# Fewer key loads, a mask built in two parts, and three moved steps in a fused decay-attention and soft-MoE kernel

## The chip, the cores and the metric

The kernel runs on one core of one Trainium2 chip. The metric is device time in microseconds, the median of several runs; lower is better.

## What is computed

Two stages follow each other. The first is block-wise linear attention with a decay `lam` of each head (batch 4, 8 heads, 768 positions, head width 64). The second is a soft mixture of experts over the 3072 tokens that come out of it (width 512, 32 slots, 8 experts of 4 slots, hidden width 1024).

```python
for b in range(nb):                       # blocks of 64 positions
    intra = einsum('bhic,bhjc->bhij', qb, kb) * Dmask          # Dmask: lam**(i-j), i >= j
    intra = einsum('bhij,bhjd->bhid', intra, vb)
    inter = einsum('bhid,bhde->bhie', qb * lam_pow, kv_state)
    out[:, :, sl] = intra + inter
    kv_state = lam_block * kv_state + einsum('bhsd,bhse->bhde', kb * rev_pow, vb)
x = out.transpose(0, 2, 1, 3).reshape(3072, 512)
logits = x @ phi                                               # 512 x 32
d = softmax(logits, over tokens);  slot_input = d.T @ x
h = relu(slot_input[e] @ w1[e]);   slot_out[e] = h @ w2[e]     # each expert e
y = softmax(logits, over slots) @ slot_out
```

## The kernel before, in words

The kernel works in chunks of 128 positions: 6 a batch element (`NB`), 24 in all (`T`). One loop over `t` (line 541) handles all of them, and every engine keeps the order in which the program issues (`InOrder`, line 52).

A chunk has three loads of 256 KB: queries and keys turned (`qT`, `kT`, head width on the partitions) and values (`vN`). Some chunks have a fourth, the keys with positions on the partitions (`kN`). `loaded(t)`, line 37, says which: before the change chunks 2, 3, 4 of every six, and 7 and 19, 14 in all. The last chunk of every six needs no such keys. For the six others `turn_k` (line 307) makes them on the chip: four TensorE transpositions of `kT` into a PSUM bank and a ScalarE copy (`kn`).

Iteration `t` issues from SyncE (SP) the loads of chunk `t+2` and, between them, part of the weight stream: 16 slabs of `w1` of 1 MB, and `w2` in nine slabs of 1 MB (`w2p`) and 28 pieces of 256 KB (`w2t`), the latter into buffers that the chunk loop no longer needs. The chunk loads share a ring of 12 buffers (`ld`).

For chunk `t` the work is:

- `scores(t)`: TensorE, keys by queries, into two banks; 8 products of 128x128 where `whole(t)`, else 16 smaller ones that leave out the upper half and store the diagonal blocks exchanged.
- `masks(t)`: VectorE multiplies the banks by the decay mask (`at`). The mask tile has six places a half: four ordinary ones, and two exchanged ones (places `HP` and `HP+1`) that only chunks which aren't `whole` read, the first of them chunk 5. `powers_of` (line 211) fills a place by a VectorE scan.
- `recall(t)`: TensorE, old state by decayed queries (`qs`, made on GpSimd by `decay_q`).
- `attend(t)`: TensorE, values by `at`, on top of `recall`; ScalarE copies the two halves out (`xt`).
- `state(t)`: TensorE, decayed keys (`kd`, made on GpSimd by `decay_k`, one buffer) by values into bank `kv`; VectorE adds the decayed state (`st`). `decay_state` on GpSimd decays it for the next chunk (`dec`).
- `natural(t)`: four TensorE transpositions of `xt` and a ScalarE copy (`x`), done for two chunks at every even `t`.
- every four chunks `logits`, `weights`, `slots` and `slot_softmax`: running softmax over the tokens.

A chunk that opens a batch element (`opens`, t = 0, 6, 12, 18) runs `state` ahead of `attend`, as odd chunks do; other even chunks run it behind. At the last chunk (`last`) a few extra products end the token softmax.

Behind the loop come the experts: `first(0)` and `first(1)` (`w1` slabs, 32 products of 512 columns each for a half of the experts and each of two banks), `second(0, ...)` and `second(1, ...)` (`w2`, for the two halves of the output columns), and `put`: a product, a copy by ScalarE or VectorE, and a 256 KB store from SP, 24 in all. The first 9 stores lie inside `second(1)`, at the places that `PUTS` names; three more of the first column half and the 12 of the second follow.

Of the kernel before, what the change touches and what calls it, by code (L numbers as in the profile page):

```python
# [16 lines left out]
NB = S // P  # L17
T = B * NB
HP = H // 2
# [16 lines left out]

def loaded(t):

    return t % NB in (2, 3, 4) or t in (7, 19)


def whole(t):
# [25 lines left out]
def decay_attn_soft_moe(  # L68
# [23 lines left out]
    def bank(tag):  # L92
        return ps.tile([P, 512], F32, tag=tag, name=tag)
# [6 lines left out]
    d = const.tile([P, P], F32, name="d")  # L100
# [3 lines left out]
    def load_chunk(t, which=(0, 1, 2, 3)):  # L104
        srcs = (qT, kT, vN, kN)
        for i in which:
            if i == 3 and not loaded(t):
                continue
            tl = loads.tile([P, 512], F32, tag="ld", name="ld")
            sp.dma_start(out=tl, in_=srcs[i][t])  # L110
            IN[t, i] = tl
# [15 lines left out]
    def load_one(pool_, tag, bufs, n=1):  # L127

        t_ = pool_.tile([P, n, 512], F32, tag=tag, name="w2t", bufs=bufs)
        for m in range(n):  # L130
            Q, x, q, i = single.pop()
            sp.dma_start(out=t_[:, m], in_=rows(Q, x, q)[i])
            wt["w2", Q, q, x, i] = t_[:, m]
# [27 lines left out]
    def load_early(n):  # L161
        for _ in range(n):
            if early:
                Q, kk, q = early.pop()
                t_ = slabs.tile([P, 2, 1024], F32, tag="slab", name="slab")
                src = w1[4 * Q + q].rearrange("k p n f -> (k p n f)").rearrange("(p n y) -> n p y", p=P, n=2)
                sp.dma_start(out=t_.rearrange("p i f -> p (i f)"), in_=src[kk])
                wt["w1", Q, q, kk] = t_
            else:
                load_two()  # L170
# [40 lines left out]
    def powers_of(places, at_zero):  # L211
        for hh in range(2):
            for y in places:
                x = hh * HP + (y if y < HP else y - 2)
                dve.tensor_tensor_scan(
                    out=mask[:, hh, y, :],
                    data0=lam_sb[:, x:x + 1].broadcast_to([P, P]),
                    data1=at_zero,
                    initial=0.0,
                    op0=ALU.mult,  # L220
                    op1=ALU.add,
                )
# [78 lines left out]
    def decay_q(t):  # L301
        if t < T and t % NB > 0:
            qs = work.tile([P, HP, P], F32, tag="qs", name="qs")
            pool.tensor_tensor(out=qs, in0=IN[t, 0].rearrange("p (a b) -> p a b", a=HP), in1=qpow, op=ALU.mult)
            QS[t] = qs

    def turn_k(t, tag="kv"):

        if t < T and t % NB < NB - 1 and not loaded(t):
            tk = bank(tag)  # L310
            for hp in range(HP):
                pe.transpose(tk[:, hp * P:(hp + 1) * P], IN[t, 1][:, hp * P:(hp + 1) * P], ident)
            kn = work.tile([P, D], F32, tag="kn", name="kn")
            act.copy(out=kn, in_=tk)
            IN[t, 3] = kn
# [37 lines left out]
    def turn_v(t):  # L353

        if t < T and not whole(t):
            v_ = IN[t, 2].rearrange("p (b h c) -> p b h c", b=2, c=DH)
            for j in range(2):
                act.copy(out=vs[64 * j:64 * j + 64], in_=v_[64 - 64 * j:128 - 64 * j, :, 2:4])
# [48 lines left out]
    def decay_state(t):  # L407
        if t % NB < NB - 2:
            st = ST["st"]
            dec = work.tile([P, HP, DH], F32, tag="dec", name="dec")  # L410
            pool.tensor_tensor(
                out=dec, in0=st, in1=lamc.broadcast_to([P, HP, DH]), op=ALU.mult
            )
            ST["dec"] = dec

    def natural(t, tag="tr"):
        tr = bank(tag)
        for hp in range(HP):
            pe.transpose(tr[:, hp * P:(hp + 1) * P], XT[t][:, hp, :], ident)
        x = keep.tile([P, D], F32, tag="x", name="x", bufs=4)  # L420
        act.copy(out=x, in_=tr)
        X[t] = x
# [59 lines left out]
    def weights(raw=True):  # L482
        dp = bank("dp")
        pe.transpose(dp[:, 0:P], e, ident)
        if raw:
            pe.transpose(dp[:, P:2 * P], L, ident)
        dve.tensor_copy(out=d, in_=dp[:, 0:P])
        return dp[:, P:2 * P]
# [52 lines left out]
    for t in range(T):  # L541
        if t + 2 < T:
            load_chunk(t + 2, (0, 1))

        want = min(NSLAB, max(0, (t * PACE + AHEAD) // 100))
        load_early(want - sent)
        sent = max(sent, want)
        if t + 2 < T:
            load_chunk(t + 2, (2, 3))
        if t == 0:  # L550
            sp.dma_start(out=L, in_=phi.rearrange("p a s -> p (a s)"))

        for _ in range((2, 4, 3)[t - T + 3] if t >= T - 3 else 0):
            load_one(*ld1)
        if t == T - 1:
            load_one(work, "kd", 1)
            load_one(work, "kn", 1)
        last = t == T - 1

        asks = t // 4 - 1 if t > 0 and t % 4 == 0 else G - 1 if last else None  # L560
        sums = t // 4 - 1 if t > 4 and t % 4 == 1 else None
        if t == 0:
            turn_k(0, "tr")
            scores(0)
            scores(1)
            turn_v(0)
        elif t > 1:
            scores(t)
        masks(t)
        if last:  # L570
            ask = logits(asks)
            next(ask)

        if t % 4 == 3 or t % 4 == 0:
            next(sm, None)
        if t == T - 1:
            next(sm, None)
        opens = t % NB == 0
        if t == 0:
            decay_k(0)  # L580
            decay_q(1)
        recall(t)
        if t > 0:
            decay_q(t + 1)
        if sums is not None:
            sm = slot_softmax(sums, weights())
        if asks is not None and not last:
            ask = logits(asks)
            next(ask)
        if t % 2 == 0 and t > 0:  # L590
            turn_k(t + 1)
            natural(t - 2)
            natural(t - 1, "dp")
        elif t % NB == NB - 1:
            turn_k(t + 1)
        if sums is not None:
            next(sm)
        if asks is not None:
            next(ask)
        if last:  # L600
            natural(t - 1)
            next(ask)

            phi4 = work.tile([P, HP, 4, SL], F32, tag="carry", name="phi4")
            four = phi_sb.rearrange("p (a o) s -> p a o s", o=1)
            pool.tensor_copy(out=phi4, in_=four.broadcast_to([P, HP, 4, SL]))
        if opens or t % 2 == 1:

            state(t)
            decay_state(t)  # L610
            if t == 0:
                turn_k(1, "tr")
        attend(t)
        if last:
            cm = bank("kv")
            pe.matmul(out=cm[:, 0:4], lhsT=blk_, rhs=gm, start=True, stop=True)
            dve.tensor_reduce(out=own, in_=cm[:, 0:4], axis=AX.X, op=ALU.min)
            weights(raw=False)
        if t == 1:
            dve.tensor_reduce(out=sel, in_=ident.rearrange("p (g s) -> p s g", g=4), axis=AX.X, op=ALU.add)  # L620
            for n in range(4):
                own_ = bass.AP(
                    tensor=ident.tensor,
                    offset=ident.offset + 16 * (n // 2) + NR * (n % 2),
                    ap=[ident.ap[0], [64, 2], [40, 2], [1, NR]],
                )
                dve.tensor_reduce(out=own4[:, n:n + 1], in_=own_, axis=AX.XYZ, op=ALU.add)
            dve.tensor_reduce(out=gsel, in_=ident.rearrange("p (g s) -> p g s", g=4), axis=AX.X, op=ALU.add)
        if not opens and t % 2 == 0:
            state(t)  # L630
        decay_k(t + 1)
        if not opens and t % 2 == 0:
            decay_state(t)
        if asks is not None and not last:
            next(ask)
        if sums is not None:
            slots(sums)
        if t == 3:
            for j in range(2):
                dve.tensor_copy(out=d[:, 64 * j:64 * j + 64], in_=ident[:, 64 - 64 * j:128 - 64 * j])  # L640
            powers_of(range(HP, HP + 2), d)
        if t == 2:
            place_phi()
        if t == 2:
            pool.tensor_copy(out=blk, in_=sel.rearrange("p (o s) -> p o s", o=1).broadcast_to([P, 4, SL]))
# [302 lines left out]
```

## Time and profile before

| | |
|---|---|
| median of 3 runs | 162.91 us (162.83 to 162.95) |
| the profiled execution's own time | 162.79 us |
| its span, first to last instruction | 161.0 us |
| TensorE busy | 143.7 us (89%) |
| VectorE / ScalarE / GpSimd busy | 90.7 / 69.3 / 70.8 us |
| moved by DMA | 62.84 MB, 390 GB/s on average |
| mean granted TensorE clock | 0.972 |

Times in the rows are microseconds from the span's start. TensorE's busy time is modelled (its products are pipelined). `sc`, `gl`, `dp`, `tr`, `kv`, `xa`, `xb` are PSUM banks; a name such as `at<-sc,mask` gives the tile that is written and those that are read. All operations are recorded on line 62, that of the helper `InOrder`.

### The profile page before, as it was taken

What the parts mean: (1) busy time and instruction counts of PE and PEld (TensorE: products, weight loads), DVE (VectorE), ACT (ScalarE), POOL (GpSimd) and SP (SyncE); (2) the same over time, 40 slices, a digit from 0 to 9 for tenths busy, and PEclk for the clock granted to TensorE, in tenths of its full rate; (3) what the DMA queues carried; (4) which work ended last, traced back from release to release, by engine and by line L of the source; (5) the groups of instructions that cost most, each with busy time, mean ns of one, the idle gap of its engine ahead of it and who ended that gap; (6) DMA issues with size and microseconds to landing.
All of it is one profiled execution on the core that took longest, in us unless ns stands there. A gap on an engine that the chain in (4) does not pass through costs nothing.

```text
span 161.0 us, 5817 instructions
## 1 busy us (share of the span) xinstructions
PE 143.7 (89%) x2397; PEld 100.3 (62%) x2397; DVE 90.7 (56%) x208; ACT 69.3 (43%) x173; POOL 70.8 (44%) x102
## 2 busy tenths in 40 slices
PE   6799997999999999989999999998999999998300
PEld 6678965687668866876868686763332465647200
DVE  1956497657585566576756476565179641327500
ACT  3132325662646475634675455633035801436400
POOL 2789692357385328586057748200003893000000
PEclk9999999999999999999999999999999999999855
DMA  4999999999999999999999999999999999999993
GB/s 166 337 402 405 414 411 417 404 416 402 413 421 408 405 412 421 415 411 404 414 406 408 415 400 407 415 393 376 388 393 414 423 413 414 407 387 356 383 383 136
DMA packets 28523, 62.84 MB, mean 390 GB/s; under 512 B 2769, under 2 KB 9041, under 8 KB 26449
## 3 DMA queue, kind: packets, MB, share of 16 engines
q1 hardware_dynamic: 28352, 62.47, 100.0%
q8 instruction: 19, 0.31, 0.7%
q14 instruction: 8, 0.06, 0.1%
q10 hardware_dynamic: 144, 0.01, 0.1%
HBM read 56.17 MB, written 6.29 MB: 388 GB/s over the span
## 4 chain that ended last, share of the span: by engine, by line
PE 66%; DMA 14%; DVE 8%; issue 2%; ACT 1%; SPq 1%; POOL 1%; DVEq 0%; ACTq 0%
PE xa L62 15%; PE sc L62 14%; DMA w2p<-w_x 11%; PE xb L62 10%; PE gl L62 9%; PE kv L62 8%; PE tr L62 6%; PE dp L62 4%; DMA ld<-kT 3%; DVE mask L62 3%; DVE o L62 2%; DVE at L62 1%; SPq L62 1%; POOL kd L62 1%; DVE acc L62 0%
## 5 line engine op out<-in xcount | busy, mean ns | idle before, releaser
L62 DVE TENSOR_TENSOR at<-sc,mask 128x512 f32<-128x512 f32 x46 | 29.6, 685 | 11.2 <-PE sc L62 9.9
L62 POOL TENSOR_TENSOR qs<-ld,qpow 128x512 f32<-128x512 f32 x20 | 25.7, 1284 | 3.4 <-POOL kd L62 2.9
L62 PEld LDWEIGHTS sc<-ld 64*64 64x64 f32 (+1 forms) x608 | 19.5, 145 | 7.5 <-issue 4.2
L62 PE MATMUL sc<-ld 64*64 64x128 f32 (+2 forms) x608 | 23.1, 257 | 1.0 <-DMA ld<-kT 0.9
L62 POOL CAST ct<-part 32x256 fp32r<-32x256 f32 x26 | 10.3, 394 | 22.6 <-DVE part L62 21.5
L62 POOL TENSOR_TENSOR kd<-ld,kpow 128x512 f32<-128x512 f32 x14 | 14.7, 1050 | 8.6 <-PE kv L62 5.0
L62 PE MATMUL kv<-ld,kd 128*64 128x64 f32 x320 | 13.6, 225 | 1.1 <-issue 0.7
L62 POOL TENSOR_TENSOR dec<-st,qpow 128x256 f32<-128x256 f32 x16 | 10.1, 628 | 10.0 <-DVE st L62 10.0
L62 PEld LDWEIGHTS kv<-ld,kd 128*64 128x64 f32 x320 | 11.5, 137 | 3.5 <-issue 1.9
L62 DVE TENSOR_TENSOR st<-dec,kv 128x256 f32<-128x256 f32 x16 | 6.7, 416 | 12.1 <-PE kv L62 12.1
L62 PE MATMUL xa<-qs,st 64*64 64x128 f32 x160 | 13.3, 277 | 0.2
L62 ACT COPY xt<-xa 128x256 f32<-128x256 f32 x24 | 8.8, 366 | 10.6 <-PE xa L62 10.6
L62 POOL TENSOR_TENSOR kd<-kn,kpow 128x512 f32<-128x512 f32 x6 | 6.3, 1042 | 15.4 <-PE xb L62 10.8
L62 PE MATMUL xb<-qs,st 64*64 64x128 f32 x160 | 12.9, 278 | 0.0
L62 PE MATMUL xa<-at,ld 128*64 128x128 f32 x132 | 12.0, 283 | 1.0 <-DVE at L62 1.0
L62 ACT COPY vs<-ld 64x256 f32<-64x256 f32 x30 | 12.1, 403 | 0.7
L62 PE MATMUL xb<-at,ld 128*64 128x128 f32 x132 | 11.4, 273 | 0.0
L62 ACT COPY x<-tr 128x512 f32<-128x512 f32 (+1 forms) x13 | 7.4, 568 | 8.3 <-PE tr L62 8.1
L62 PEld LDWEIGHTS xa<-qs,st 64*64 64x64 f32 x160 | 9.0, 132 | 1.8 <-issue 0.9
L62 ACT COPY xt<-xb 128x256 f32<-128x256 f32 x23 | 8.6, 374 | 0.9
L62 ACT COPY lq<-gl 128x512 f32<-128x512 f32 (+1 forms) x6 | 3.4, 569 | 12.8 <-PE gl L62 11.9
L62 PEld LDWEIGHTS xa<-at,ld 128*64 128x64 f32 x132 | 6.8, 136 | 3.3 <-DVE at L62 1.9
(154 smaller groups left out, 273.4 us busy)
## 6 DMA issues: line engine op xcount, KB each, us to landing
slab<-w_x SPq DMA_DIRECT2D x16, 1024.0 KB, 8.7
w2p<-w_x SPq DMA_DIRECT2D x9, 1024.0 KB, 13.8
w2t<-w_x SPq DMA_DIRECT2D x28, 256.0 KB, 5.1
ld<-qT SPq DMA_DIRECT2D x24, 256.0 KB, 6.9
ld<-kT SPq DMA_DIRECT2D x24, 256.0 KB, 6.7
ld<-vN SPq DMA_DIRECT2D x24, 256.0 KB, 7.0
y<-o SPq DMA_DIRECT2D x24, 256.0 KB, 3.9
ld<-kN SPq DMA_DIRECT2D x14, 256.0 KB, 7.7
```

What stands on the lines that cost most here:

```text
L62: return self._tc.keep_in_program_order(f(*args, **kwargs))
```

## The change

Four edits.

1. `loaded(t)` names chunks 2 and 4 of every six and chunks 7 and 19: ten chunks. Chunks 3, 9, 15 and 21 get their natural keys from `turn_k` (called at `t` = 2, 8, 14 and 20, into bank `kv`), and their four loads of 256 KB are gone.
2. The exchanged mask places are filled in two parts: the two copies that make `d` move from the end of chunk 3 to that of chunk 1, place `HP` is scanned at the end of chunk 2 and place `HP+1` at the end of chunk 3.
3. At openings other than the first (t = 6, 12, 18) `decay_k(t + 1)` is issued ahead of `decay_state(t)` on GpSimd, not behind it.
4. At the last chunk `natural(t - 1)` is issued behind `weights(raw=False)`, the transposition of `e`, and not ahead of `attend`.

```diff
 def loaded(t):
-    return t % NB in (2, 3, 4) or t in (7, 19)
+    return t % NB in (2, 4) or t % (2 * NB) == 7
@@
         if last:
-            natural(t - 1)
             next(ask)
@@
         if opens or t % 2 == 1:
             state(t)
-            decay_state(t)
+            if t == 0 or not opens:
+                decay_state(t)
             if t == 0:
                 turn_k(1, "tr")
         attend(t)
@@
             weights(raw=False)
+            natural(t - 1)
@@
         if not opens and t % 2 == 0:
             state(t)
         decay_k(t + 1)
-        if not opens and t % 2 == 0:
+        if t > 0 and t % 2 == 0:
             decay_state(t)
@@
-        if t == 3:
+        if t == 1:
             for j in range(2):
                 dve.tensor_copy(out=d[:, 64 * j:64 * j + 64], in_=ident[:, 64 - 64 * j:128 - 64 * j])
-            powers_of(range(HP, HP + 2), d)
+        if t in (2, 3):
+            powers_of((HP + t - 2,), d)
```

## Rows read from the trace of the kernel before

**Rows 1.** The page: busy tenths of TensorE and DMA in 40 equal slices.
```profile
PE   6799997999999999989999999998999999998300
DMA  4999999999999999999999999999999999999993
```
**Rows 2.** The chain that ended last, 143:161: start, duration, what.
```profile
125.57 17.99 DMA w2p<-w_x
```
**Rows 3.** Busy time by stretch: window, length, then busy time (instructions) of each engine.
```profile
111.82:143.34 31.52, 31.52 (x391) 14.58 (x391) 15.49 (x35) 10.49 (x23) 10.25 (x26) 1.00 1.04 405
143.34:143.60 0.26, 0.00 (x0) 0.00 (x0) 0.00 (x0) 0.00 (x0) 0.00 (x0) 1.00 1.09 386
```
**Rows 4.** Timeline of SP: the eleventh and the last store (start, duration, engine, operation).
```profile
147.24 0.57 SPq L62 DMA_DIRECT2D y<-o  x1
...
156.04 0.58 SPq L62 DMA_DIRECT2D y<-o  x1
```
**Rows 5.** Issue to landing, us: the last store, and the first load.
```profile
DMA to landing us min/median/max: 3.9/3.9/3.9
...
DMA to landing us min/median/max: 2.7/2.7/2.7
```
**Rows 6.** The DMA view of 150:161: GB/s in 40 slices of 0.275 us.
```profile
GB/s 384 384 387 380 387 380 391 373 391 384 376 395 372 395 369 395 380 384 387 373 395 376 391 376 387 384 376 395 376 235 82 71 71 74 22 0 0 0 0 0
```
**Rows 7.** Timeline of ScalarE: the copy that the eleventh store sends.
```profile
146.17 0.59 ACT L62 COPY o<-tr 128x512 f32<-128x512 f32 x1
```
**Rows 8.** DMA issues: name, count, KB each, median us to landing.
```profile
ld<-kN SPq DMA_DIRECT2D x14, 256.0 KB, 7.7
w2t<-w_x SPq DMA_DIRECT2D x28, 256.0 KB, 5.1
```
**Rows 9.** The chain in chunk 12: a turn of keys, then a natural transposition.
```profile
57.20 0.59 PE kv L62 x4
57.79 0.44 PE tr L62 x4
```
**Rows 10.** Groups by shape: the mask scans (count, busy us, mean ns, idle before).
```profile
L62 DVE TENSOR_TENSOR_SCAN mask<-lam_sb,ident 128x128 f32<-128x128 f32 x8 | 3.2, 474 | 2.4 <-DMA lam_sb<-lam_x 2.4
L62 DVE TENSOR_TENSOR_SCAN mask<-lam_sb,d 128x128 f32<-128x128 f32 x4 | 4.6, 1205 | 0.0
```
**Rows 11.** Timeline of VectorE, from chunk 3 to chunk 4.
```profile
18.67 1.29 DVE L62 TENSOR_TENSOR at<-sc,mask 128x512 f32<-128x512 f32 x2 [0.58 <-PE sc L62]
...
20.75 4.59 DVE L62 TENSOR_TENSOR_SCAN mask<-lam_sb,d 128x128 f32<-128x128 f32 x4
25.27 1.26 DVE L62 TENSOR_TENSOR at<-sc,mask 128x512 f32<-128x512 f32 x2
```
**Rows 12.** Timeline of GpSimd in the same stretch.
```profile
17.70 1.04 POOL L62 TENSOR_TENSOR kd<-ld,kpow 128x512 f32<-128x512 f32 x1 [1.21 <-PE kv L62]
18.70 0.63 POOL L62 TENSOR_TENSOR dec<-st,qpow 128x256 f32<-128x256 f32 x1
...
20.64 1.26 POOL L62 TENSOR_TENSOR qs<-ld,qpow 128x512 f32<-128x512 f32 x1
```
**Rows 13.** Timeline of TensorE in chunk 4: the first half of `attend`.
```profile
25.98 0.66 PE L62 MATMUL xa<-at,ld 128*64 128x128 f32 x8 [0.98 <-DVE at L62]
```
**Rows 14.** Waits of the whole span: TensorE's weight loads for decayed keys.
```profile
PEld kv L62 <- POOL kd L62: 1.3, 4, 0.5
```
**Rows 15.** Chunk 21's decayed keys (GpSimd, TensorE), then its `kN` load's issue and landing.
```profile
94.65 1.04 POOL L62 TENSOR_TENSOR kd<-ld,kpow 128x512 f32<-128x512 f32 x1 [2.60 <-PE sc L62]
...
95.75 0.69 PE L62 MATMUL kv<-ld,kd 128*64 128x64 f32 x16 [0.27 <-POOL kd L62]
...
L62 SPq DMA_DIRECT2D ld<-kN x1: 328/328/328, 85.8 to 85.8; - x1
...
DMA to landing us min/median/max: 8.7/8.7/8.7
```
**Rows 16.** Timeline of ScalarE in the last chunk: its copy for `natural(22)`.
```profile
106.22 0.56 ACT L62 COPY x<-tr 128x512 f32<-128x512 f32 x1
```

## The prediction

> **What bounds the kernel now.** I read the page's busy tenths first, then the chain that ended last, then busy time by stretch, then the timelines of SP, VectorE, GpSimd and TensorE at the places that the diff touches. The tenths show two engines that are full at once: DMA at 9 from the second slice to the end, TensorE at 9 nearly to the end [rows 1]. So a share of busy time can't say which of them sets the end; the tail must. The chain waits there for the last `w2` slab, which was issued at 125.57 and took 17.99 us to land, at 143.56 [rows 2]. That looks like a kernel bound by bytes. But TensorE had worked for 31.52 of the 31.52 us before 143.34, and waited only 0.26 us for that slab [rows 3]. The two streams arrive together: if the loads end 2.5 us earlier, TensorE is next, 0.26 us behind. That is the main reading, and the reason why I don't take the saved bytes for the gain.
>
> Behind the loads come 24 stores. The eleventh was issued at 147.24, the last at 156.04 [rows 4]; 13 steps of 0.68 us, each a 0.58 us instruction of SP and a little around it. So once the eleventh is out, the rest follows at SP's pace. The last one landed 3.9 us after its issue, at 159.95 [rows 5], and 1.05 us of closing work ends the span of 161.0. The end is therefore: issue of the eleventh store, plus 8.8 us, plus the landing time, plus 1.05. The issue goes by the copy that fills the store, which ended at 146.17 + 0.59 = 146.76 [rows 7], at the end of TensorE's tail.
>
> **What a landing costs when nothing queues.** 3.9 us is not the price of a store by itself. DMA moved 370 to 395 GB/s for 29 slices, up to 158.0, in the next 235 (about three fifths of a slice, so to 158.15), and then for 1.3 us 71 to 82 GB/s [rows 6], a fifth of the full rate: most of the 16 DMA engines had finished 2.1 us behind the last issue, and a few worked off a queue that the loads had left them. Data ended near 159.55, 0.4 us before the landing. A store that meets no queue should land 2.1 + 0.4 = 2.5 us behind its issue (estimate); the first load of the kernel, of the same size, took 2.7 [rows 5]. I take 2.6, with 2.5 and 3.9 as ends. 2.6 is nearer to both rows of an empty queue; 3.9 holds if the few slow engines keep a queue whatever is issued.
>
> **The change part by part.**
>
> Four `kN` loads of 256 KB are gone. The 24 stores of the same size go at 0.68 us each, loads a little faster: 4 x 0.63 = 2.5 us of DMA, so loads would end near 141.1 instead of 143.56. SP issues four instructions fewer; nothing new is queued there. Does DMA stay fed when TensorE falls back? Loads land 7.7 us behind their issue in the loop and 5.1 in the `w2t` stretch [rows 8], against 2.7 unloaded: a queue of 5.0 and 2.4 us. DMA running 2.5 us ahead and buffers freed up to 1 us later use 3.5 us of it. In the loop that is covered. In the `w2t` stretch up to 1.1 us could be lost, which puts the end of loads at 142.2 at worst, still ahead of TensorE. I cost it at nothing.
>
> Four turns of keys are added on TensorE. A turn in chunk 12 costs 0.59 us and the four transpositions next to it 0.44; the difference is the change of product that any first group pays [rows 9]. A turn goes in front of two others, so 4 x 0.44 = +1.76 us. Each adds a ScalarE copy of 0.59 us behind which the copies of `natural` and `xt` queue; ScalarE is 43% busy and chunk 12 shows the same sequence without a wait of TensorE, so nothing. The keys are copied before `state` wants bank `kv`.
>
> The scans. Today all four lie behind chunk 3 and take 4.59 us; `at` of chunk 4 starts at 25.27 for it [rows 11], and TensorE sits idle for 0.98 us in front of `attend` [rows 13]. This idle time is all that can be won. In the new order two scans stand on VectorE in front of `at` of chunk 3, where only 0.58 us was idle [rows 11]; `attend(3)` waits for that, and with it all that TensorE has queued. What does a scan cost there? Alone or beside short GpSimd operations 0.47 us, beside chunk 3's long ones 1.2 us [rows 10]. GpSimd runs `kd` from 17.70 to 18.74 and `dec` to 19.33 at that place [rows 12], so the long price applies, less what has run already: the first scan ends some 0.3 us behind `kd`, the second some 0.3 us behind a `dec` lengthened by 0.1, at 19.7 (+0.44 for the turn) instead of 18.09. `at` of chunk 3 starts 1.0 us later, `attend(3)` 0.9 us later by its own margin: +0.88. Bounds: two scans of 0.47 (wait 0.3) and two of 1.2 (wait 1.8). The other two scans end near 23.4, well ahead of 25.27, and TensorE reaches `attend(4)` at 25.00 + 0.44 + 0.88 = 26.3 without idling: -0.98.
>
> Here the Trainium skill speaks against the edit: "SBUF — State Buffer", section "Who interferes with whom", says that a VectorE instruction with two SBUF inputs and a GpSimd instruction that reads SBUF exclude each other for a whole instruction, by order of issue. By it the scans of chunk 2 pay the long price, as chunk 3's rows show; without it they would cost 0.47 each and the time would come out 0.6 us lower, at 161.1.
>
> Openings: `kd` ahead of `dec`. TensorE's weight loads wait 1.3 us in four places for `kd` [rows 14]; two of the four are openings' successors, chunks 7 and 19. `kd` no longer stands behind a `dec` of 0.63 us [rows 12]; `dec` now stands behind a `kd` of 1.04, and the first to want it is the next chunk's `st`, behind 16 products on TensorE that wait for that `kd` themselves. -0.3, a little under the four waits' mean for each of the two (0 to -0.5).
>
> Chunk 21: its `kd` started at 94.65, when its `kN`, issued at 85.8, had landed 8.7 us later, and TensorE idled 0.27 us [rows 15]. Turned keys are there earlier: -0.3 (0 to -0.4).
>
> The last transposition: ScalarE's copy of 0.56 us at 106.22 stands ahead of the `xt` copy that the last logits want [rows 16]. Behind `e` it no longer does; but the other half of `xt` is copied by VectorE, which the edit leaves as it is, and the transpositions still precede those logits on TensorE. So less than half of the copy: -0.2 (0 to -0.3).
>
> Sum on TensorE up to the experts: 1.76 + 0.88 - 0.98 - 0.3 - 0.3 - 0.2 = +0.86 us. The wait of 0.26 for the last slab goes: +0.6 at the tail. The eleventh store is ready at 146.76 + 0.6 = 147.4, issued then (147.24 today), and lands 2.6 later at 150.0 instead of 151.1: -1.1. The profiled execution took 162.79, so 161.7; the median of the runs is 0.12 above it, which I leave in the rounding. Half of what the bytes promise goes to TensorE, and what is won comes from a shorter queue at the stores.
>
> **The rivals.**
>
> Bytes alone. If TensorE's terms come out at their low ends (1.76 - 0.98 - 0.5 - 0.4 - 0.3 + 0.3 - 0.26, about -0.4), the eleventh store is ready at 146.4 and lands at 149.0, and the stores follow the loads: 162.8 - 2.1 to 2.5, about 160.5. For it: [rows 2]. Against it: TensorE's 31.52 full microseconds [rows 3].
>
> The landing stays at 3.9. Then the eleventh store lands at 147.4 + 3.9 = 151.3, as today: 162.9, no change. For it: the last 13 stores land at an even 3.9. Against it: the drop of the rate at 158.15 [rows 6].
>
> TensorE pays all. Place: chunks 2 to 4 and the tail. If the two scans cost 1.2 each behind chunk 2 (wait 1.8) and openings, chunk 21 and the end give nothing back, the sum is 1.76 + 1.8 - 0.98 - 0.26 = +2.3; the store lands at 149.1 + 2.6 = 151.7 and the time is 163.4, slower. It decides from a net delay of 1.7 us at the eleventh store (148.5, 2.6 before today's landing at 151.1).
>
> **How the numbers follow.** Forecast 161.7, chance 0.58; bytes alone 160.5, 0.14; landing unchanged 162.9, 0.16; TensorE pays all 163.4, 0.12. Measurements of this kernel tell 0.2% (0.33 us) from no change. Faster: 0.58 + 0.14 = 0.72; same 0.16; slower 0.12. The range takes in bytes alone and the unchanged landing, 160.3 to 163.0, and leaves out the slower case.
>
> **What would show each step.** Loads: the last `w2p` should land near 141.1 and TensorE no longer wait for it. Turns: there should be ten copies `kn` instead of six, each with four transpositions. Scans: `at` of chunk 3 near 20.1, of chunk 4 near 23.5, TensorE without idle time in front of `attend(4)`. Chunk 21: no wait of `state` for `kd`. `first(0)` should start 0.9 us later than 111.82. Stores: a dip of DMA's rate around the tenth store and landings under 3 us behind it. I am wrong if the experts start over 1.7 us later, or if stores still land 3.9 us behind their issue.

## The result and the profile after

The changed kernel takes 161.49 us (median of 5 runs, 161.14 to 162.37) against 162.95 us (162.83 to 163.25) for the kernel before: a ratio of 0.991, 95% interval 0.9882 to 0.9939. Timed again, beside two of the experiments, it took 161.23 us against 162.96 us (0.990, 0.9868 to 0.9933). The profiled execution took 161.60 us, its span 159.8 us; before it was 162.79 and 161.0. So it is faster by 1.5 to 1.7 us. 161.7 was forecast, and the time fell well inside the range. The way there was another one, though. Ratios leave out executions over 1.5% above the fastest of the same kernel; medians don't.

The page's busy tenths, as in [rows 1], show both engines full again:

```profile
PE   6999989999999999989999999998999999998400
DMA  5999999999999999999999999999999999999994
```

The chain that ended last, 126:160 (start, duration, what), has no load in it any more. [rows 2] had the last `w2` slab with 17.99 us; now TensorE's own products follow each other to the copies that fill the stores. It stops at the last of those, at 150.73, and so can't say what sets the last landing at 158.84:

```profile
126.39 6.91 PE kv L62 x128
133.30 1.73 PE xa L62 x32
...
142.28 1.91 PE xa L62 x32
147.05 3.08 DVE o L62 x5
```

Busy time by stretch, the counterpart of [rows 3]: TensorE is busy for all of the 32.31 us from the start of the experts to the end of its `w2` products, and the idle 0.26 us is gone.

```profile
111.83:142.21 30.38, 30.38 (x376) 13.96 (x376) 14.87 (x35) 9.66 (x22) 10.25 (x26) 1.00 1.02 397
142.21:144.14 1.93, 1.93 (x34) 1.00 (x33) 0.62 (x1) 0.84 (x2) 0.00 (x0) 1.00 1.08 371
```

The experts start at 111.83, where they started at 111.82 before. The last `w2p`, issued at 125.58, landed at 141.40, and the last store was issued at 155.16. The two landings, from the views of those loads and stores, answer to 17.99 in [rows 2] and to 3.9 in [rows 5]:

```profile
L62 SPq DMA_DIRECT2D w2p<-w_x x1: 2098/2098/2098, 125.6 to 125.6; - x1
DMA to landing us min/median/max: 15.8/15.8/15.8
...
L62 SPq DMA_DIRECT2D y<-o x1: 589/589/589, 155.2 to 155.2; - x1
DMA to landing us min/median/max: 3.7/3.7/3.7
```

ScalarE's copy for the eleventh store ends at 146.23 (146.76 in [rows 7]), and that store goes out at 146.34 (147.24 in [rows 4]):

```profile
145.64 0.59 ACT L62 COPY o<-tr 128x512 f32<-128x512 f32 x1
```

So the loads end 2.16 us earlier, the stores from the eleventh on go out 0.9 us earlier, and a store still lands 3.7 us behind its issue, where 2.6 had been forecast.

### The profile page after: what moved, and what is told of

The parts are those of the page before. It is cut to its first block, busy times and chain, and to the rows that moved or that the text cites. A ratio compares the mean times of both kernels' runs of the same rounds, so it can differ in the third digit from the quotient of the medians.

```text
span 159.8 us, 5845 instructions
## 1 busy us (share of the span) xinstructions
PE 145.2 (91%) x2413; PEld 102.0 (64%) x2413; DVE 90.8 (57%) x208; ACT 71.2 (45%) x177; POOL 70.8 (44%) x102
## 4 chain that ended last, share of the span: by engine, by line
PE 81%; DVE 8%; DMA 2%; issue 2%; POOL 1%; ACT 0%; DVEq 0%; POOLq 0%
PE xa L62 20%; PE kv L62 14%; PE sc L62 14%; PE xb L62 11%; PE gl L62 11%; PE tr L62 7%; PE dp L62 5%; DVE mask L62 3%; DVE o L62 2%; DMA lam_sb<-lam_x 2%; DVE at L62 1%; POOL kd L62 1%; DVE acc L62 0%; DVEq L946 0%; DVE cs L62 0%
## 5 line engine op out<-in xcount | busy, mean ns | idle before, releaser
L62 POOL TENSOR_TENSOR kd<-kn,kpow 128x512 f32<-128x512 f32 x10 | 10.4, 1043 | 26.6 <-PE xb L62 14.1
L62 POOL TENSOR_TENSOR kd<-ld,kpow 128x512 f32<-128x512 f32 x10 | 10.5, 1053 | 3.1 <-PE kv L62 3.1
L62 PEld LDWEIGHTS xb<-qs,st 64*64 64x64 f32 x160 | 8.7, 132 | 1.1 <-issue 0.9
```

The costliest lines, as they stand in the source:

```text
L62: return self._tc.keep_in_program_order(f(*args, **kwargs))
```

## Which chain ends last

Two accounts of the end were put against each other. Theory A is the prediction's: TensorE's tail fills the eleventh store, SP issues 13 more at 0.68 us each, and the last one lands. By theory B, called D in the last run, the DMA engines set the end: the last load, then 24 stores at the pace at which the engines work them off. Then the time from issue to landing is no price at all, but what is left of the queue. Theory C says that the gain is TensorE's shorter waits, and not the bytes.

**Edit 1 alone** (14 loads become 10, the other three edits undone).

```diff
-    return t % NB in (2, 3, 4) or t in (7, 19)
+    return t % NB in (2, 4) or t % (2 * NB) == 7
```

> Edit 1 alone: ten key loads, four more turns; scans, openings and last transposition as before. Theory A (the end is set by TensorE's tail, the 14 last stores at SP's pace of 0.68 us and their landing; bytes count only as far as the last weight slab makes TensorE wait): four turns add 1.76 us on TensorE, one of them (0.44) falls into the idle microsecond of chunk 4, and chunk 21's wait of 0.3 to 0.4 goes, so first(0) starts near 112.8 (before 111.82, after 111.83); the wait for the last slab goes too (-0.5), so the eleventh store is ready about 0.5 us later than before: 162.3 to 162.9 us. Theory B (bytes set the end, the other three edits are idle): the whole gain is here, 161.2 to 161.7.

Measured: 162.06 us, ratio 0.9949 (0.9921 to 0.9977), between the two theories. The last load landed at 141.56, as early as in the whole change. But in the profiled execution the experts started at 113.47, 1.65 later than before, and the last store was issued at 157.25 and landed at 160.31. Here TensorE was the later of the two. This execution took 163.05 us, 1.0 above the median, and had a pause of 1.10 us in chunk 8 that the profile names "issue", so by how much TensorE is later in the others stays open.

**Edits 2 to 4 alone** (14 loads stay).

> Edits 2 to 4 without edit 1: 14 key loads as before. Theory A: TensorE comes out of the chunk loop earlier (first(0) near 110.8, from the waits that vanish), but the last weight slab lands at 143.5 as before, and TensorE waits for it for about 1.3 us instead of 0.26: 162.8 to 163.0, no change. Theory B: 162.9, no change too, with the same wait. Theory C (the gain is TensorE's waits, not bytes): 161.4 to 162.2.

Measured: 163.03 us, ratio 1.0007 (0.9984 to 1.0031). No gain without the bytes; C falls. The experts started at 111.70, where A wanted 110.8; the last load landed at 143.81.

**All four edits, and the bytes too:** the four loads are made again, and nobody reads them.

```diff
-            if i == 3 and not loaded(t):
+            if i == 3 and not loaded(t) and t % NB != 3:
```

> After, but the four natural-key loads are still made (into buffers that nobody reads): bytes of before, TensorE's work of after. Theory A and B: the last slab lands near 143.6 to 143.9 again, TensorE waits for it by 0.3 to 0.5 us, SP's stores meet a longer queue: 162.6 to 163.0, the gain is gone. Theory C (bytes are idle, the three moved steps bring the gain): 161.5.

Measured: 163.04 us, 1.0007 (0.9983 to 1.0030). The last load landed at 143.75. Without the four loads gone nothing is gained. (They take their places in the ring of buffers again, too; the run doesn't separate these from the bytes.)

**The change without its four turns** (chunks 3, 9, 15 and 21 decay the keys of the chunk before instead, so their states are not the reference's).

```diff
+        if t < T and t % NB == 3:
+            IN[t, 3] = IN[t - 1, 3]
+            return
...
```

> After, but chunks 3, 9, 15 and 21 decay the natural keys of the chunk before them, so their four turns (16 transpositions, 4 copies) are left out and their state is not that of the reference; bytes as after. Theory A: TensorE is 1.0 to 1.7 us earlier at first(0) (110.1 to 110.8), and the end then falls back to what the loads allow: last slab at 141.4 as after, 24 stores of 0.68 behind it: 160.3 to 160.7. Theory B (bytes set the end already): 161.5, as after, with TensorE waiting over 1 us for the last slab.

Measured: 160.64 us, 0.9871 (0.9836 to 0.9906). The experts started 1.62 us earlier than with the change, at 110.21: four turns cost 4 x 0.41 us. The loads ended 0.13 us earlier, at 141.27, and the last store, issued 1.42 us earlier, landed 3.9 us behind its issue:

```profile
L62 SPq DMA_DIRECT2D y<-o x1: 588/588/588, 153.7 to 153.7; - x1
DMA to landing us min/median/max: 3.9/3.9/3.9
```

The time is in A's range (160.3 to 160.7) and not at B's 161.5. That speaks for TensorE's tail counting, too, once the bytes are gone, though the interval overlaps that of the change.

**The kernel before, with 1.1 us more of TensorE's time in the tail.** For the kernel before, A could still be held up to here. This run moves the tail alone: three products more ahead of the last two groups of `w2` products.

```diff
+    def idle():
+        rep = bank("xb")
+        for _ in range(3):
+            pe.matmul(out=rep[:, 0:HD], lhsT=blk_, rhs=so[:, 0:HD], start=True, stop=True)
+
+    fill[14] = idle
     second(1, po1, fill)
```

> The kernel before, with three more products of 128x128 by 128x256 (results unused) put on TensorE between the last products with the last w2 slab: about 1.3 us, behind which all that the last stores need is queued. Theory A (the end is the issue of the eleventh store plus 13 steps and a landing of about 3.9, so TensorE's tail sets it): the eleventh store is issued about 0.8 us later (its copy is ready 1.3 us later, and 0.48 us of that was spent behind SP's tenth store), and the time is 163.6 to 163.9 us. Theory D (the end is the landing of the last load plus 24 stores at 0.68 us on the slowest DMA engine; landings behind the issue are only what is left of that queue): stores are issued later but land when they did, the last landing is still 16.4 us behind the last load's, its distance from the issue falls from 3.9 to about 3.1, and the time stays within 0.2 us of 162.95.

Measured: 162.75 us against 162.73, ratio 0.9992 (0.9971 to 1.0012): nothing, where A wants 163.6 to 163.9. The timeline of TensorE shows the added products, and the views of the last `w2p` and of the last store their landings:

```profile
143.22 1.56 PE L62 MATMUL xb<-so,blk 128*128 128x256 f32 x6
```
```profile
L62 SPq DMA_DIRECT2D w2p<-w_x x1: 4733/4733/4733, 125.5 to 125.5; - x1
DMA to landing us min/median/max: 18.7/18.7/18.7
...
L62 SPq DMA_DIRECT2D y<-o x1: 590/590/590, 156.7 to 156.7; - x1
DMA to landing us min/median/max: 3.9/3.9/3.9
```

TensorE ended its `w2` products 1.11 us later than before (145.78), and the eleventh store went out at 147.89 instead of 147.24. In this execution the last load landed at 125.54 + 18.65 = 144.19, and the last store 16.39 us behind that, at 160.58. In the kernel before it was 143.56 and 159.95: 16.39 us as well. This trace alone would fit A too: it is of the slowest of the twelve executions (163.38 us), its last load landed 0.63 us later than before and its eleventh store went out 0.65 us later, so that the landing stayed at 3.9, where D had expected 3.1. What A can't explain is the median. Nor can it explain the two kernels above that have all the bytes: their last stores were issued at 156.03 and 155.85, no later than before (156.04), and landed 4.2 and 4.3 us behind. For the kernel before, A falls; there the stores follow the loads.

That gives a rule which can be tried on the other traces. In the kernel before, 24 stores land 0.682 us apart, the first 0.69 us behind the last load: the DMA chain ends at the last load + 16.38. The other chain is the last issue plus a landing without a queue, 2.5 us (the landing of the first three stores in the run without late loads, below). All numbers are microseconds from the span's start:

| kernel | last load | + 16.38 | last issue + 2.5 | last landing |
|---|---|---|---|---|
| before | 143.56 | 159.94 | 158.54 | 159.95 |
| changed | 141.40 | 157.78 | 157.66 | 158.84 |
| changed, once more | 141.94 | 158.32 | 158.13 | 158.34 |
| edit 1 alone | 141.56 | 157.94 | 159.75 | 160.31 |
| edits 2 to 4 alone | 143.81 | 160.19 | 158.53 | 160.20 |
| change and bytes | 143.75 | 160.13 | 158.35 | 160.15 |
| change without turns | 141.27 | 157.65 | 156.24 | 157.67 |
| scans late | 140.80 | 157.18 | 156.32 | 157.18 |
| openings as before | 141.59 | 157.97 | 157.66 | 158.88 |
| natural ahead | 143.33 | 159.71 | 158.69 | 159.72 |
| before, tail late | 144.19 | 160.57 | 159.16 | 160.58 |

In eight of these eleven the last landing is the DMA chain's, to 0.02 us (the first of them gave the constant). Edit 1 alone is the one in which the other chain is later. In the changed kernel the two lie within 0.2 us of each other (157.78 and 157.66, once more 158.32 and 158.13): by the rule both set its end, and shortening one alone gains next to nothing. (Without the turns the later sum is 0.13 us lower than in the changed kernel, the median 0.6 to 0.85; the execution without turns lost nothing among its stores.) The two that are left, the changed kernel and the one with its openings as before, end 0.9 to 1.1 us behind both chains. They are next. Three traces that come below are not in the table: without late loads the last landing is 1.0 us behind the other chain, with two queues for the stores 1.2 us behind it, and with two queues and late scans it is the DMA chain's (160.82 for 160.81).

## What holds up the DMA engines by a microsecond

In the changed kernel's trace the first three stores landed 0.74, 1.39 and 2.05 us behind the last load, as the rule wants; the fourth landed 1.86 us behind the third, not 0.68, and all the rest 0.68 apart again. The views of the third and of the fourth store:

```profile
L62 SPq DMA_DIRECT2D y<-o x1: 576/576/576, 140.0 to 140.0; - x1
DMA to landing us min/median/max: 3.5/3.5/3.5
...
L62 SPq DMA_DIRECT2D y<-o x1: 743/743/743, 140.7 to 140.7; - x1
DMA to landing us min/median/max: 4.7/4.7/4.7
```

1.18 us were lost there. The DMA view of 142.8:143.85 shows what else was on the engines: one packet of 16 KB that fetches instructions, which took 5.6% of 16 engines for 1.05 us, 0.95 us of one engine.

```profile
q1 hardware_dynamic: 395, 0.38, 103.5%
q8 instruction: 1, 0.02, 5.6%
```

The page counts 19 of these in the span, one every 6 us or so in the loop, and 4826 instructions of TensorE (2413 products and as many weight loads): one packet for every 254. The Trainium skill's "Runtime: NRT & Kernel Launch", section "Instruction fetch mechanics", has blocks of 16 KB, 256 instructions each, that an engine's sequencer fetches by itself; size and number agree, so I take these for TensorE's. The Trainium skill calls the cost of a block "mostly hidden"; for TensorE it was, which the trace shows busy for all of the 32.31 us that held four of them, but for the transfers beside it it was not here. At the end of the store stretch one engine seems to lag. The DMA view of 150:161 (slices of 0.275 us): the full rate to 157.1, then 22 to 26 GB/s, about a sixteenth of it, for a microsecond more, where [rows 6] had a fifth.

```profile
GB/s 376 395 376 387 376 391 380 384 391 372 398 373 384 384 384 387 373 402 373 391 384 376 387 373 399 372 168 26 22 26 19 0 0 0 0 0 0 0 0 0
```

Are the 3.7 us of the last landing, then, what the loads have left (theory Lb), or such a delay among the stores (theory La)? **The changed kernel without its last four slabs** tells it (the second half of the output columns uses the `w2` slabs of the first, so half of the output is not the reference's):

```diff
...
-    while units:
-        load_two()
+    units.clear()
```

> The changed kernel without the last four w2 slabs (4 MB); the second half of the output columns uses the w2 slabs of the first half, so its values are not the reference's. Loads end near 131.5 us instead of 141.4, so no load is queued when the stores go out. Theory La (the landing of 3.7 us at the end comes from one DMA engine held up during the stores, by a fetch of instructions of about 1 us, and not from the loads): stores land 2.4 to 2.7 us behind their issue until that fetch, and 3.3 to 3.7 behind it, as SP issues them as fast as an engine works them off; the last store's landing is over 3.3 us and the time is 161.2 to 161.6. Theory Lb (it is what the loads' queue left over): landings of 2.4 to 2.7 us to the end, and the time is 160.3 to 160.6 us.

Measured: 161.30 us, 0.9899 (0.9877 to 0.9921), La. The loads ended at 131.00, and the engines stood idle when the stores began. The third, the fourth and the last store:

```profile
L62 SPq DMA_DIRECT2D y<-o x1: 587/587/587, 140.0 to 140.0; - x1
DMA to landing us min/median/max: 2.5/2.5/2.5
...
L62 SPq DMA_DIRECT2D y<-o x1: 589/589/589, 140.7 to 140.7; - x1
DMA to landing us min/median/max: 4.4/4.4/4.4
...
L62 SPq DMA_DIRECT2D y<-o x1: 587/587/587, 155.0 to 155.0; - x1
DMA to landing us min/median/max: 3.5/3.5/3.5
```

2.5 us without a queue, as the prediction had worked out; 4.4 from the store on that met the fetch (142.1 here, 1.40 us long), and from there on stores land 0.68 us apart to the end, so what was lost isn't caught up. Ten microseconds of loads less bring 0.2 us against the first timing of the change (161.49) and none against the second (161.23). So it isn't the loads' end alone, either, on which the changed kernel's time hangs: without any late load the other chain ends at 155.04 + 2.5 = 157.54, 0.1 us earlier than with them.

**The changed kernel once more** shows the other outcome.

> The changed kernel once more, beside the two others on the same chip: 161.3 to 161.7 us. Its chunks 2 to 5 take 14.3 us again (13.8 with late scans); whatever idle time of TensorE named issue there is in chunks 8 and 15 to 19 differs from the first execution's 0 and 0.82 us.

Measured: 161.23 us, 0.990 (0.9868 to 0.9933). In its profiled execution there was a fetch at 142.0 too, but no step of the stores is longer than 0.74 us, and the last store landed as forecast:

```profile
L62 SPq DMA_DIRECT2D y<-o x1: 586/586/586, 155.6 to 155.6; - x1
DMA to landing us min/median/max: 2.7/2.7/2.7
```

So a fetch may cost 1.0 to 1.9 us or nothing. The loads show the same. Their lead over the kernel before was 2.0 us at the `w2t` that landed at 114.38; the next one landed 2.06 us behind it, and the lead fell to 0.6. The fourth `w2p` brought it back to 2.3, because there the kernel before lost 1.4 us. The views of those loads, first the two `w2t` of the changed kernel:

```profile
L62 SPq DMA_DIRECT2D w2t<-w_x x1: 328/328/328, 109.4 to 109.4; - x1
DMA to landing us min/median/max: 5.0/5.0/5.0
...
L62 SPq DMA_DIRECT2D w2t<-w_x x1: 328/328/328, 110.0 to 110.0; - x1
DMA to landing us min/median/max: 6.4/6.4/6.4
```

and of the kernel before, the third and the fourth `w2p`:

```profile
L62 SPq DMA_DIRECT2D w2p<-w_x x1: 379/379/379, 118.5 to 118.5; - x1
DMA to landing us min/median/max: 8.7/8.7/8.7
...
L62 SPq DMA_DIRECT2D w2p<-w_x x1: 515/515/515, 119.0 to 119.0; - x1
DMA to landing us min/median/max: 12.0/12.0/12.0
```

Beside both lies a fetch. The DMA views, of 113.9:116 for the changed kernel and of 128.6:130.6 for the kernel before (the share is of 16 engines):

```profile
q8 instruction: 1, 0.02, 2.7%
```
```profile
q8 instruction: 1, 0.02, 3.0%
```

All fourteen traces bear this out. From 20 us on, 36 of 1876 landings of queued transfers came over 0.8 us later than their usual step. Beside 35 of the 36, at most 2.5 us ahead of the step, lay one of these packets, beside the last an 8 KB packet of another engine's fetch; of all landings 57% have one so near. But only 35 of the 252 fetches of that time have such a step beside them. That is a coincidence in time, shown many times; no run changes the fetches and nothing else.

The account of the 1.1 us between the two profiled executions is therefore: 2.0 us of lead by the bytes, less 1.4 at 114 us, plus 1.4 at 129 us, less 1.2 among the stores, plus 0.3 of small steps. From 110 us on the changed kernel's execution paid for two fetches and that of the kernel before for one. Without them the loads of the two would end 2.2 us apart, but not the kernels: the kernel before would end near 159.95 - 1.4 = 158.55, the changed one by its other chain near 157.66, and the difference would be 0.9 us (an estimate). The traces don't tell which engine a fetch falls on, so why some count and others (two of the changed kernel's four behind 110 us, three of the four of the kernel before) cost nothing stays open; nor can a kernel be given without them.

**Are the 0.68 us SP's or the engines'?** In the page's slices loads came at 400 to 420 GB/s, stores at 384. Six of the last twelve stores were issued from ScalarE, behind its own copies:

```diff
-        sp.dma_start(out=dst.rearrange("(p i) c -> p i c", i=2), in_=o[:, :, cols])
+        q = act if half == 1 and nput[0] % 2 == 1 else sp
+        q.dma_start(out=dst.rearrange("(p i) c -> p i c", i=2), in_=o[:, :, cols])
```

> The changed kernel with six of the last twelve stores issued from ScalarE, behind its own copies, instead of SP. Theory A (from the eighth store on SP's own instructions, one every 0.68 us, set the end): the 256 KB loads ran at 400 to 430 GB/s, the stores at 380 to 388, so the engines have up to 0.06 us a store to give; the last store lands 0.3 to 0.8 us earlier and the time is 160.7 to 161.2 us. Theory S (380 to 388 GB/s is what stores to memory take, whoever issues them): stores are issued earlier but land no earlier, the landing of the last grows from 3.7 to 5 us and more, and the time stays at 161.5 us.

Measured: 161.83 us, 0.9926 (0.9898 to 0.9953): no gain, as S has it, but not by S's way, since the last landing stayed at 3.7 us. Stores that met a queue landed 0.6 to 0.75 us apart however they were issued. ScalarE, which now spends 0.54 to 0.62 us on each of its stores, fell behind with its copies, so that the rate sagged. **The same with the scans behind chunk 3:**

> The changed kernel with its scans behind chunk 3, as in the run with late scans, and six of the last twelve stores issued from ScalarE. Theory A: chunks 2 to 5 take 0.5 us less, the tail gets 0.3 to 0.8 us shorter: 160.3 to 160.9 us. Theory S: 161.0 to 161.5 us, as with late scans alone.

Measured: 161.92 us, 161.3 for the four executions in the ratio, 0.9908 (0.9873 to 0.9944): no gain over late scans alone (161.24). In its profiled execution, of 163.55 us, the loads ended late (144.43), so that a queue stood, and the 24 stores landed 0.683 us apart from both queues as they do from one. The kernel before says the same: its first nine stores, all over 4.6 us behind their issue, landed 0.68 us apart however unevenly SP issued them. So the 384 GB/s are the stores' own.

## The three small edits

TensorE's time from the start of one chunk's `sc` products to that of another's, from the traces, microseconds; "issue" are pauses of TensorE for which the profile shows no cause, taken out where the head says so:

| kernel | chunks 2 to 4 | 5 to 7 | 14 | 15 to 19, without issue | 21 | 23 to the experts |
|---|---|---|---|---|---|---|
| before | 14.35 | 10.43 | 3.78 | 18.93 | 4.54 | 9.81 |
| changed | 14.28 | 10.40 | 4.22 | 18.95 | 4.21 | 9.43 |
| scans early, no turns | 13.81 | 10.40 | 3.78 | | 5.02 | 9.46 |
| scans late | 13.79 | 10.40 | 4.22 | 18.95 | 4.21 | 9.44 |
| openings as before | 14.29 | 10.43 | 4.22 | 18.98 | 4.21 | 9.46 |
| natural ahead | 14.28 | 10.40 | 4.21 | 18.95 | 4.21 | 9.82 |

("Scans early, no turns" is edits 2 to 4 alone; its 5.02 in chunk 21 holds a longer wait for `kd`.) In chunk 14, which has a turn and nothing else new, the turn costs 0.44 us.

**Scans behind chunk 3, as before, on top of the change.**

```diff
-        if t == 1:
+        if t == 3:
             ...
-        if t in (2, 3):
-            powers_of((HP + t - 2,), d)
+            powers_of(range(HP, HP + 2), d)
```

> The changed kernel with all four scans of the exchanged masks, and the copies that make d, back behind chunk 3. Theory A (the scans moved a wait and cost or gain little): the idle time of about 1.0 us in front of attend(4) is back, the 0.5 us in front of attend(3) is gone; the experts start 0 to 0.5 us later than with the change, and the end moves with them: 161.4 to 162.0 us. By the prediction's own term (0.88 paid at chunk 3 against 0.98 won at chunk 4) it is 0.1 us. Theory B (the bytes alone set the end): last load and last store stay where they are, 161.5 us.

Measured: 161.24 us, 0.9917 (0.9887 to 0.9946), the same as the change within the interval. But chunks 2 to 4 are 0.49 us shorter with late scans, and the idle time in front of `attend(4)` is not back. This was in no expectation. The timelines of VectorE and GpSimd in that kernel show why:

```profile
20.65 3.58 DVE L62 TENSOR_TENSOR_SCAN mask<-lam_sb,d 128x128 f32<-128x128 f32 x4
24.15 1.26 DVE L62 TENSOR_TENSOR at<-sc,mask 128x512 f32<-128x512 f32 x2
...
20.74 1.40 POOL L62 TENSOR_TENSOR qs<-ld,qpow 128x512 f32<-128x512 f32 x1
22.10 0.74 POOL L62 TENSOR_TENSOR dec<-st,qpow 128x256 f32<-128x256 f32 x1
22.80 1.15 POOL L62 TENSOR_TENSOR kd<-ld,kpow 128x512 f32<-128x512 f32 x1
```

Four scans took 4.59 us in the kernel before [rows 11] and 3.58 here. There the first scan started at 20.75, 0.11 us behind GpSimd's `qs` [rows 12], and each of the four sat out one GpSimd operation. Here it starts at 20.65, 0.09 us ahead of `qs`, and only three do. Edit 1 alone, which has the turn and late scans too, repeats it (first scan 0.09 us ahead of `qs`, 3.58 us in all, chunks 2 to 4 in 13.79), and so does the kernel before with its tail late (0.11 us behind, 4.59). It is this order that the Trainium skill's "SBUF — State Buffer", section "Who interferes with whom", speaks of: the two engines exclude each other for whole instructions, and whoever comes first goes first. The traces agree; the scans' price depends on 0.2 us of order. With the turn, TensorE and all behind it come 0.44 us later at chunk 3, and the scans fall into the better order by themselves. Without the turn, moving them early wins 0.54 us (14.35 to 13.81); with the turn it loses 0.49.

**Openings as before, on top of the change.**

```diff
-            if t == 0 or not opens:
-                decay_state(t)
+            decay_state(t)
...
-        if t > 0 and t % 2 == 0:
+        if not opens and t % 2 == 0:
```

> The changed kernel with the state's decay ahead of the keys' decay again at openings. Theory A (TensorE's chain sets the start of the experts): the waits of 0.25 to 0.3 us for decayed keys are back at chunks 7 and 19, the experts start 0.2 to 0.5 us later, and the time is 161.6 to 162.0 us. Theory B (later slack swallows them, or the bytes alone set the end): waits are back, but the experts start within 0.1 us of the changed kernel's, 161.5 us.

Measured: 161.38 us, 0.9896 (0.9869 to 0.9924), the same. TensorE's weight loads wait 0.33 us for `kd` at chunks 7 and 19 again, but chunks 5 to 7 and 15 to 19 are only 0.03 us longer each. In the changed kernel the same loads stand idle for 0.17 us of "issue", so half of each wait is there in any case.

**The last natural transposition ahead, on top of the change.**

```diff
         if last:
+            natural(t - 1)
             next(ask)
...
             weights(raw=False)
-            natural(t - 1)
```

> The changed kernel with the last chunk's natural transposition ahead of attend again. Theory A: the last chunk takes 0.1 to 0.5 us longer from its scores to the start of the experts (the prediction's term was 0.2, the changed kernel's trace suggests 0.37), and the time is 161.6 to 162.0 us. Theory B (bytes alone set the end): 161.5 us whatever the last chunk does.

Measured: 162.08 us, 0.9935 (0.9912 to 0.9958), against 0.991 and 0.990 for the change; the intervals overlap. The last chunk takes 0.39 us longer. The timelines of TensorE, first of the change, then with `natural` ahead, where the logits wait for ScalarE's copy of `xt`:

```profile
106.47 0.39 PE L62 MATMUL kv<-gm,blk 128*128 128x4 f32 x2 [0.30 <-DVE gm L62]
106.71 0.31 PE L62 MATMUL dp<-ident,e 128*128 128x128 f32 x1
106.85 0.60 PE L62 MATMUL tr<-ident,xt 128*128 128x128 f32 x4
107.29 1.06 PE L62 MATMUL sc<-xt,phi 128*128 128x128 f32 x8
```
```profile
106.71 0.31 PE L62 MATMUL dp<-ident,e 128*128 128x128 f32 x1
107.36 0.91 PE L62 MATMUL sc<-xt,phi 128*128 128x128 f32 x6 [0.34 <-ACT xt L62]
```

In that execution the loads ended at 143.33, with a step of 3.98 us between two `w2p` (2.48 elsewhere) beside a fetch at 135.5, so its trace can't say how much of the 0.6 us between the medians is the edit's.

## Why the prediction came out, and where it was wrong

**The number was right, and two of its terms were wrong by a microsecond each in opposite directions.** "The eleventh store is ready at 147.4, and lands 2.6 later at 150.0" was the last step. It was ready at 146.23, issued at 146.34 and landed 3.63 later, at 149.97. That the two cancelled is luck. In the second execution (161.05 us) they didn't: the store was ready at 146.01, went out at 146.81 and landed 2.70 later, at 149.51.

**The first step was wrong for the kernel before: "the end is therefore: issue of the eleventh store, plus 8.8 us, plus the landing time".** It took the 3.9 us of [rows 5] for a price that an emptier queue would lower, and TensorE's tail for the place where the end is decided. The prediction had the right observation: a few engines work off a queue that the loads have left, and a store without one lands in 2.5 us (2.5 measured). It followed from that observation that a later issue costs nothing as long as the queue lasts: the kernel before had 159.94 - 158.54 = 1.4 us of it. 1.1 us more of TensorE work moved nothing. Issue and landing are not two prices that add; the end is the later of two sums, the last load + 16.38 and the eleventh store's issue + 8.8 + 2.5. With the prediction's own terms (141.1 and 147.4) these are 157.5 and 158.7. The second is later, and by its landing of 2.6 the prediction had it almost to the digit, so the wrong step did its forecast no harm: the rule with the same terms gives 161.5 us.

The harm lies in TensorE's sum. With 0.0 instead of +0.86 the eleventh store is ready at 146.5, the two sums are 157.5 and 157.8, and the time is 160.6: the number of "bytes alone", whose condition was met (ready at 146.4 forecast, 146.23 measured), and which was given 0.14. The profiled execution with late scans, whose loads ended at 140.80 and whose stores lost nothing, took 159.9 us, the fastest of its eight. What lies between 160.6 and the measured 161.2 to 161.5 is, as far as the traces tell, the loads' end at 141.4 to 141.9 instead of 141.1, and the fetches, which no term had.

A smaller step was wrong too: the issue doesn't go by the copy alone. SP's instruction for an earlier store was stretched, and the eleventh went out 0.48 us behind its copy in the kernel before, 0.11 in the changed one and 0.80 in its second execution.

**TensorE's sum: +0.86 forecast, 0.0 measured** at the start of the experts. By its terms:
- Turns: 0.44 each, as forecast; the ten copies `kn` are there.
- Scans: `at(3)` started at 20.14 and `at(4)` at 23.54 (20.1 and 23.5 forecast), and `attend(4)` no longer waits. But `attend(3)` waited 0.53 us, not 0.88, and chunks 2 to 4 with their turn came out 0.07 us shorter instead of 0.34 longer. That the turn by itself takes the idle time of [rows 13] away, as edit 1 alone shows, the sum did not see: it added two edits that share a cover.
- Openings: 0.03 each instead of 0.3 for the two. (The prediction's words, a little under the mean of 0.33 for each of the two, would give 0.6; its sum has 0.3.) The waits went from 0.33 to 0.17 us, the time didn't follow; the prediction's bound of 0 held, its value did not.
- Chunk 21: 0.33, forecast 0.3.
- The last transposition: 0.38, forecast 0.2 with 0.3 as the end. The logits' whole wait for `xt` went.
- The first `sc` products of chunk 8 took 1.63 us in the execution of before and 1.16 in this one. They vary between executions of kernels that don't differ there (1.36 with the tail late, 1.58 without late loads, 1.16 in the changed kernel's second), and the 0.47 us account for half of the difference.

**Loads**: the last `w2p` at 141.40 for a forecast 141.1, and TensorE no longer waits for it. Without this term there is no gain (163.04 us). But TensorE's sum stands beside it: edit 1 alone, which leaves TensorE later, takes 162.06 us, the change without its four turns 160.64.

**Landing unchanged** was given 0.16 and in the profiled execution it nearly was (3.68 against 3.91), with the other term making up for it; in the second execution it was 2.70. With 3.68 the prediction's own sign of being wrong, stores that still land 3.9 us behind their issue, was nearly there. **TensorE pays all** is the way that edit 1 alone points (experts 1.65 us later in its profiled execution, with a pause of 1.10; 162.06 us). That the other three edits keep TensorE off the end is likely from that, but the intervals of the two kernels overlap.

No version that computes the same beats the changed kernel beyond its interval: late scans, 161.24 us, are as fast, with 0.5 us less of TensorE's time in chunks 2 to 4 and a simpler order.

## What to carry to other kernels

Before counting on a landing time, add up the transfers behind the last load: where the last landing is the last load's plus so many stores at their own pace, the time from issue to landing is a remainder, and work that is moved ahead of the issue costs and wins nothing until the queue is gone. Then the last issue plus a landing without a queue takes over, so work out both and take the later. Two edits that remove the same idle time must be costed together and in both orders. And of one execution against another, compare the lead of equal transfers along the whole run, since delays of a microsecond each can hide a lead of two.

## What the runs showed of the hardware

- Instruction fetches run on the DMA engines beside the kernel's transfers: 16 KB, 0.9 to 1.5 us of one engine, 19 in the span. Landings jumped by 0.8 to 2.0 us beside 35 of 252 of them.
- Stores of 256 KB are worked off one in 0.68 us (384 GB/s) whoever issues them; `w2t` loads of the same size land 0.62 us apart.
- SP's store instruction is now and then stretched while stores are behind. Its durations in the changed kernel, min/median/max in ns, are below; the longest was the seventh store's, when landings were at 4.4 us. How far behind they are doesn't decide it: in the kernel before, the second and third store, 5.6 us behind, took 0.56 and 0.58 us, the tenth, 4.5 us behind, 1.27.

```profile
L62 SPq DMA_DIRECT2D y<-o x24: 561/587/1385, 138.6 to 155.2; - x24
```

- Four VectorE scans, the first of which starts 0.09 us ahead of a GpSimd operation instead of 0.11 us behind it, took 3.58 us instead of 4.59.
